# A mixed attention and gMLP kernel: Q's first tile in two halves, a finer warm-up, and new limits for the planner

## The chip, the cores and the metric

The kernel runs on one NeuronCore of a Trainium2 chip. The core has five engines that work side by side, each through its own instructions in order: TensorE (PE, with its weight loads shown apart as PEld), VectorE (DVE), ScalarE (ACT), GpSimd (POOL) and SyncE (SP), which here only issues DMAs. They wait for each other through semaphores. The metric is the device time of one execution in microseconds; lower is better. The kernel before takes 730.46 us, the median of three runs between 730.2 and 732.36.

## The reference, cut to what matters

One input x of 2048 rows and 512 columns goes through two branches, which are mixed row by row:

```python
def _A_ref(x, wq, wk, wv, wo):            # H = 32 heads, Dh = 16, one K and one V for all heads
    q = (x @ wq).reshape(B, S, H, Dh).transpose(0, 2, 1, 3)
    k = x @ wk
    v = x @ wv
    scores = jnp.einsum('bhqd,bkd->bhqk', q, k) * Dh ** (-0.5)
    p = _softmax(scores, axis=-1)
    o = jnp.einsum('bhqk,bkd->bhqd', p, v)
    return o.transpose(0, 2, 1, 3).reshape(B, S, H * Dh) @ wo

def _B_ref(x, w_in, w_sp, b_sp, w_out):   # F = 1376, Fh = 688
    z = _gelu(jnp.einsum('bsd,df->bsf', x, w_in))
    z1 = z[..., :Fh]
    z2 = _layernorm(z[..., Fh:], axis=-1)
    g = jnp.einsum('ts,bsf->btf', w_sp, z2) + b_sp[None, :, None]
    return jnp.einsum('bsf,fd->bsd', z1 * g, w_out)

g = _sigmoid((x * gate_w).sum(-1, keepdims=True))
return g * _A_ref(...) + (1 - g) * _B_ref(...)
```

Nearly all the work outside the matrix products is the softmax: 32 heads times 2048 times 2048 exponentials.

## The kernel before, in words

**Tiles.** The scores are computed with keys on the 128 partitions and queries along the free axis. A block is one product of 128 keys by 512 queries for one head; it fills one of the eight PSUM banks. Four heads of a group sit on four strips of 32 rows of the array, so four score products run side by side. A unit is 512 queries, one group of four heads and one of the two head parities: 32 units of 64 blocks (16 key tiles, four heads), 2048 blocks in all. x is loaded transposed in four chunks of 512 rows, in the order `XO = (0, 3, 2, 1)`; Q is made in 16 tiles of 128 columns by 512 queries (`g_Q`, line 463), K in chunks of 512 keys (`g_K`, line 419; the first chunk as 128 and 384), V in chunks of four key tiles (`g_V`, line 481).

**Who does the exponential.** Most blocks go to ACT: one activation (line 770) takes two or three banks out of PSUM and writes them as bf16 weights into a ring of 19 slots. The banks of its two alternating sets are 2, 3, 4 and 0, 1 (`EB`). Other blocks go to DVE, in batches of four (one key tile of one unit, four heads): it copies a block out of PSUM with a scale and an offset (`d_A`, line 782), squares it (`d_u`, line 789), and squares the result once more (`d_w`, line 795); this last step is done by DVE or by POOL, in pieces of 256 columns. Each block of DVE costs PE two products with V instead of one, and each unit gets a few correction products (`KTV`, `SVB`). DVE's blocks come through banks 5 and 4 (`DBK`); bank 4 is shared with ACT's set of three. Banks 6 (`BO`) and 7 (`BM`) hold the output sums of a unit and everything else.

**What sets the order.** The order of instructions on each engine is fixed when the program is built. A planner (from line 372) keeps a clock for PE, ACT and DVE with a fixed cost for every operation and for every arrival (the table `T`, lines 893 to 899), and always lets the engine with the earliest clock pick its next instruction (`pe_step`, `act_step`, `dve_step`; the loop is at line 1693). PE prefers scores for ACT when a set of banks is free, then score blocks for DVE, then products with V, then other work (`fill_pick`, line 1191). While the clock is below `HEAD` and the list `first` is not empty, PE takes that list's work right after the scores (lines 1414 to 1417). When PE has been too idle, the planner inserts products with zeros.

**The limits of the planner.** They stand in `PR` (line 57) and in constants above it. `RLAST` is how many blocks of the last unit must be left over when DVE takes another batch (line 989), and whether DVE may have the shared bank there (line 1376). `FLEX` is the backlog of DVE, in planned ns, below which it may take the shared bank. `WIN` is how much PSUM work DVE must have before it for POOL to be given a piece of 512 columns (line 1598) or one of its long operations (line 1589). `WRES` and `IDR`, `IDN` govern when DVE takes second products itself: it leaves `WRES` pieces of 256 columns to POOL, and when idle takes up to `IDN` pieces if at least `IDR` are there. `PRESS` is the number of free slots of the ring below which products with V are urgent.

**The head.** Memsets on DVE and POOL come first. `WARM` products on a constant tile CT (line 364) keep PE busy until x arrives. SP issues the loads of x, ACT's queue those of wk, the first quarter of wq, wv and the gate weight. DVE builds the replicated wk (line 327) and the first tile of wq (`wq_tile`, line 331), POOL the other three. The list `first` (line 902) starts with K of the first 128 keys, Q tile 0, the rest of K, and V of the chunk; the first scores need the first K piece and Q tile 0, whole.

**The tail.** When the last unit's sums are whole, DVE transposes them out of PSUM (line 807), normalises, transposes back (line 838), PE does the last output products, DVE and ACT scale, and SP sends the rows out.

Of the kernel before, what the change touches and what calls it, by code (L numbers as in the profile page):

```python
# [16 lines left out]
DH = 16  # L17
# [9 lines left out]
NMAX = 8  # L27
# [13 lines left out]
NZ = 22  # L41
WARM = 12
RLAST = 16
XO = (0, 3, 2, 1)
N0 = 3
A_OV = 63.3
HEAD = 45000.0
C_TN = 1250.0
GATE = 20000.0
# [117 lines left out]
def build_kernel(nc, x_d, wq_d, wk_d, wv_d, wo_d, win_d, wsp_d, bsp_d, wout_d, gw_d, out_d):  # L167
    es = ExitStack()
    with es:
# [83 lines left out]

        op("dve", lambda v: v.memset(CT[:], 1.0 / 64.0), w=["CT"])
        for e in range(2):
# [3 lines left out]
        op("dve", lambda v: v.memset(good[:], 1.0), w=["good"])  # L259
        op("dve", lambda v: v.memset(KTV[:], 0.0), w=["KTV"])  # L260
        op("pool", lambda g: g.memset(KN[:], 0.0), w=["KN"])
# [18 lines left out]
        def nonc(fn):  # L280
            def f(q):
                with nc.allow_non_contiguous_dma(reason="small"):
                    return fn(q)
            return f

        def ld_x(c):
# [44 lines left out]
        def wq_tile(eng, t, key, raw):  # L331
            for e in range(2):
                op(eng, lambda v, e=e: v.tensor_copy(wqd[:, :, t, :].rearrange("p a (g e d) -> p a g e d", e=2, d=DH)[:, :, :, e, :],
                                                     wq_raw[:, :, 128 * t + 64 * e:128 * t + 64 * e + 64].rearrange("p a (g d) -> p a g d", d=DH)),
                   r=[raw], w=[key])
# [4 lines left out]
        op("pool", lambda g: g.memset(bspz[:], 0.0), w=[("bspz", 0), ("bspz", 1)])  # L340
        op("pool", lambda g: g.memset(wout[32:64, 5, :], 0.0), w=["wout5"])
# [3 lines left out]
        op("pool", lambda g: g.memset(z2[:, NST * FH:], 0.0), w=["z2pad"])  # L345
        op("dve", lambda v: v.memset(sel0[:], 0.0), w=["sel0"])
        op("dve", lambda v: v.memset(sel0[:, 16:18], 1.0), w=["sel0"])
        op("dve", lambda v: v.transpose(sel[:], sel0[:]), r=["sel0"], w=["sel"])

        def mm(dst, lhsT, rhs, start, stop, r, w, tp=None, chan=None, tag=""):  # L350
# [68 lines left out]
        def g_K(c, lo=0, hi=512, e=0, b=BM):  # L419
            key = "K0a" if c == XO[0] and lo == 0 and e == 0 else ("K%d" % e, c)  # L420

            def piece(dt):
                return lambda: fm(b, hi - lo, 0, wk_r[e][:, dt, :], xT[:, dt, 512 * c + lo:512 * c + hi], dt == 0, dt == 3, [("wk_rep", e), ("x", c), ("z1", 5)], "K")

            def ev():
                op("dve", lambda v: v.tensor_copy(KA[:, e, 512 * c + lo:512 * c + hi], bank(b, hi - lo)), r=[bkey(b)], w=[key], tag="Kev")  # L426
# [36 lines left out]
        def g_Q(q, b=BM):  # L463
            c, t = q // 4, q % 4

            def piece(dt):
                return lambda: fm(b, 512, 0, wqd[:, dt, t, :], xT[:, dt, 512 * c:512 * c + 512], dt == 0, dt == 3,
                                  ["wqd0" if t == 0 else "wqd", ("x", c)], "Q")

            def ev():  # L470
                op("dve", lambda v: v.tensor_copy(QA[:, q % NQ, :], bank(b)), r=[bkey(b)], w=[("Q", q % NQ)], tag="Qev")  # L471
# [5 lines left out]
            return Group([(C_MM, piece(dt)) for dt in range(4)], [(C_EV, ev)],  # L477
                         lambda: when(("x", c), "wqd" if t else "wqd0", *([("Qdone", 2 * (q - NQ)), ("Qdone", 2 * (q - NQ) + 1)] if q >= NQ else []),
                                      *([("QSfree", q - 2)] if q >= 2 else [])), done, bank=b, tag="Q")

        def g_V(c, b=BM):
            nw = 2 * DH + 1
            kn = 4 * c + 4 > NKT - NMAX

            def piece(k, dt):
                t0 = 512 * c + 128 * k
                return lambda: fm(b, nw, 64 * k, xT[:, dt, t0:t0 + 128], wvg[:, dt, 0:nw], dt == 0, dt == 3, ["wv", "gw", "wvk", ("x", c)], "V")
            src = bank(b, 256).rearrange("p (k w) -> p k w", w=64)
# [84 lines left out]
        def g_z1(ft, tc):  # L573
            def piece(dt):
                return lambda: fm(BM, 512, 0, win[:, dt, 128 * ft:128 * ft + 128], xT[:, dt, 512 * tc:512 * tc + 512], dt == 0, dt == 3,
                                  ["win", ("x", tc)], "z1")
            ev = lambda: op("dve", lambda v: v.tensor_copy(z1[:, ft, 512 * tc:512 * tc + 512], bank(BM)), r=[bkey(BM)], w=[("z1", ft)], tag="z1ev")
            return Group([(C_MM, piece(dt)) for dt in range(4)], [(C_EV, ev)], lambda: when("win", ("x", tc)), setT(("z1", ft, tc)), tag="z1")

        def g_z2(st, h):  # L580
            def piece(dt):
                return lambda: fm(BM, 344, 0, xT[:, dt, 128 * st:128 * st + 128], win[:, dt, FH + 344 * h:FH + 344 * h + 344], dt == 0, dt == 3,
                                  ["win", ("x", st // 4)], "z2")
            ev = lambda: op("dve", lambda v: v.tensor_copy(z2[:, FH * st + 344 * h:FH * st + 344 * h + 344], bank(BM, 344)),
# [307 lines left out]

        T["wqd0"] = 6400.0
        T["wqd"] = 17000.0
        T["x0"] = 0.0
# [262 lines left out]
        def add_checks(now):  # L1158
            pu = st_["pu"]
            if pu < NU and st_["ua"] > pu:  # L1160
# [14 lines left out]
                elif "SVB" in T and not pv_const[pu]:  # L1175
                    pv_const[pu] = True
                    for g in range(4):
                        add_item(pu, g, (max(now, T["SVB"]), lambda last, g=g, n=n: o_mm(pu, g, SVB[:, NMAX - n, :], CT[:], ["SVB", "CT"], last), None, None))
            if pu < NU and pu not in chk_added:
# [59 lines left out]
        def pe_step(now):  # L1239
            r = pe_work(now)  # L1240
            if r is None:
# [4 lines left out]
                if now > 20000.0 and b < (W_GEL if gst["arm"] and gst["t"] > now - 8000.0 else pr["W_MIN"]) * W_WIN:  # L1246
# [3 lines left out]
                    if (topen is None or t_end + 40.0 <= lim) and (ds is None or ds > t_end):  # L1250
# [6 lines left out]
                        if zb is not None:  # L1257
                            for g in range(4):
                                mm(ps[32 * g:32 * g + 32, 512 * zb:512 * zb + 512], zer[:, 32 * g:32 * g + 32], CT[:], zb == BM, zb == BM, ["zer", "CT"], [bkey(zb)],
                                   tp=(0, 32 * g), chan="p" if zb == BO else None, tag="warm")  # L1260
# [36 lines left out]
        def dz_emit(cur, c_p):  # L1297
# [7 lines left out]
            if i < 20:  # L1305
                ft, tc = i // 4, i % 4
                fm(b, 512, 0, win[:, dt, 128 * ft:128 * ft + 128], xT[:, dt, 512 * tc:512 * tc + 512], dt == 0, dt == 3, ["win", ("x", tc)], "z1")
                t_end = c_p + C_MM
            else:
                tc = 2 * (i - 20) + pos // 4  # L1310
                o = 512 * b + 256 * (pos // 4)
                for q in range(4):
                    c0 = 512 * tc + 256 * (q // 2)
                    mm(ps[32 * q:32 * q + 32, o:o + 256], win[:, dt, 640 + 32 * (q % 2):672 + 32 * (q % 2)], xT[:, dt, c0:c0 + 256], dt == 0, dt == 3,
                       ["win", ("x", tc)], [bkey(b)], tp=(0, 32 * q), tag="z1")
                t_end = c_p + C_256
# [21 lines left out]
        def pe_work(now):  # L1338
# [550 lines left out]
```

## Time and profile before

| | |
|---|---|
| median of 3 runs | 730.46 us (730.2 to 732.36) |
| the profiled execution's own time | 732.71 us |
| its span, first to last instruction | 730.6 us |
| mean granted TensorE clock | 0.994 |
| busy: PE, DVE, ACT, POOL | 712.7, 704.5, 711.4, 467.0 us |
| ACT, exponentials over two banks | 725, 668.1 us busy |
| ACT, exponentials over three banks | 15, 23.1 us busy |

A row of the timeline gives the start from the beginning of the span, the duration, the engine, the line of the kernel, the operation, output and input, the shape and how many instructions were merged; a bracket gives the idle time of the engine before it and what ended that. A row of the groups gives all instructions of one line, engine and shape: count, busy time in us, mean ns of one, and the idle time before them. Almost all PE work has one line, 354, since a helper records it; there the tiles tell the groups apart.

### The profile page before, as it was taken

To read this page: it belongs to the slowest core of one execution; us is meant where nothing else is said; L and a number is where in the kernel's file an instruction comes from. 1 tells how busy PE (TensorE), PEld (TensorE's weight loads), DVE (VectorE), ACT (ScalarE), POOL (GpSimd) and SP (SyncE) were. 2 spreads that over 40 slices of the span, in tenths; PEclk is the share of its full clock that TensorE was granted. 3 is DMA by queue.
4 is the path that set the end of the run, shared out by engine and by line. 5 is a ranking of instruction groups with operands and counts; after the bars stand their busy time and mean duration, and the time that the engine had idled before them with its cause. 6 is when DMAs were issued, how large, how long until landed. Compare 5 with 4: busy or idle time off the path is not lost.

```text
span 730.6 us, 21786 instructions
## 1 busy us (share of the span) xinstructions
PE 712.7 (98%) x9037; PEld 208.4 (29%) x9037; DVE 704.5 (96%) x1035; ACT 711.4 (97%) x760; POOL 467.0 (64%) x437
## 2 busy tenths in 40 slices
PE   8999999999999999999999999999999999999995
PEld 3322333323422223222222322222232222222321
DVE  6799999999999999999999999999999999999994
ACT  5999999999999999999999999999999999999994
POOL 5834667661177777776676777767776567668660
PEclk9999999999999999999999999999999999999997
DMA  8341000000000001400000050000005000000001
GB/s 170 125 96 24 2 2 2 1 3 2 2 2 2 1 2 20 99 23 9 2 1 2 3 117 22 10 2 2 2 7 112 15 17 2 2 2 2 2 2 33
DMA packets 48609, 17.29 MB, mean 24 GB/s; under 512 B 44180, under 2 KB 47992, under 8 KB 48504
## 3 DMA queue, kind: packets, MB, share of 16 engines
q1 hardware_dynamic: 46392, 15.67, 9.3%
q8 instruction: 72, 1.18, 0.7%
q10 hardware_dynamic: 2112, 0.17, 0.2%
q14 instruction: 33, 0.27, 0.1%
HBM read 3.25 MB, written 2.10 MB: 7 GB/s over the span
## 4 chain that ended last, share of the span: by engine, by line
PE 71%; ACT 17%; DVE 6%; issue 5%; DMA 1%; ACTq 0%; DVEq 0%
PE ps L354 71%; ACT P L770 16%; DVE UW L782 2%; DVE UW L789 1%; DMA xT<-in_A_x_dram 1%; ACT z L1327 1%; DVE UW L795 1%; DVE bst L598 0%; ACT z L592 0%; DVE km L453 0%; DVE KA L426 0%; DVE T L807 0%; ACT L592 0%; DVE outsb L697 0%; DVE QA L471 0%
## 5 line engine op out<-in xcount | busy, mean ns | idle before, releaser
L770 ACT ACTIVATE P<-ps 128x1024 bf16<-128x1024 f32 (+1 forms) x741 | 686.2, 1182 | 5.9 <-PE ps L354 5.6
L795 POOL TENSOR_TENSOR UW<-UW 128x512 f16<-128x512 f16 (+1 forms) x281 | 363.5, 1294 | 161.2 <-DVE UW L795 67.3
L782 DVE TENSOR_SCALAR UW<-ps 128x512 f16<-128x512 f32 (+1 forms) x424 | 346.1, 837 | 2.5 <-PE ps L354 1.4
L354 PE MATMUL ps<-QA,KA 32*128 32x512 bf16 x2048 | 312.4, 384 | 6.1 <-ACT P L770 2.9
L354 PE MATMUL ps<-P,V 128*32 128x512 bf16 x1496 | 212.4, 385 | 0.4 <-issue 0.2
L354 PEld LDWEIGHTS ps<-QA,KA 32*128 32x128 bf16 x2048 | 84.7, 91 | 308.6 <-ACT P L770 153.5
L789 DVE TENSOR_TENSOR UW<-UW 128x2048 f16<-128x2048 f16 (+1 forms) x163 | 171.4, 1054 | 0.6
L354 PE MATMUL ps<-UW,VW 128*32 128x512 f16 x552 | 118.8, 384 | 0.0
L354 PE MATMUL ps<-wT,z 128*32 128x512 bf16 (+1 forms) x1536 | 116.2, 366 | 0.0
L795 DVE TENSOR_TENSOR UW<-UW 128x1024 f16<-128x1024 f16 (+5 forms) x167 | 108.0, 661 | 0.2
L354 PE MATMUL ps<-UW,V 128*32 128x512 f16 x552 | 84.2, 384 | 0.2 <-DVE T L807 0.2
L354 PEld LDWEIGHTS ps<-P,V 128*32 128x32 bf16 x1496 | 49.1, 94 | 57.4 <-issue 51.6
L475 POOL TENSOR_TENSOR QSQ<-QA 128x512 bf16<-128x512 bf16 x16 | 28.9, 1806 | 22.9 <-DVE z L612 7.0
L354 PEld LDWEIGHTS ps<-wT,z 128*32 128x32 bf16 x1536 | 27.7, 94 | 42.6 <-issue 42.0
L354 PEld LDWEIGHTS ps<-UW,VW 128*32 128x32 bf16 x552 | 28.1, 94 | 14.9 <-issue 11.6
L354 PE MATMUL ps<-wout,z 128*32 128x512 bf16 x384 | 31.6, 384 | 0.0
L354 PE MATMUL ps<-win,xT 128*32 128x344 bf16 x512 | 30.8, 312 | 0.1
L830 POOL TENSOR_TENSOR Tn<-T,rc 128x512 bf16<-128x512 f32 x15 | 24.6, 1639 | 6.4 <-DVE UW L782 3.1
L807 DVE STREAM_TRANSPOSE T<-ps 128x512 f32<-128x512 f32 (+1 forms) x33 | 22.6, 688 | 4.1 <-PE ps L354 4.1
L354 PE MATMUL ps<-QA,KTV 128*32 128x512 bf16 x128 | 25.0, 384 | 0.0
L354 PE MATMUL ps<-CT,SVB 128*32 128x512 bf16 x128 | 24.6, 384 | 0.0
L354 PEld LDWEIGHTS ps<-UW,V 128*32 128x32 bf16 x552 | 19.9, 94 | 15.5 <-issue 11.5
(116 smaller groups left out, 378.5 us busy)
## 6 DMA issues: line engine op xcount, KB each, us to landing
out_dram<-outsb SPq DMA_DIRECT2D x16, 128.0 KB, 1.7
win<-in_B_w_in_dram SPq DMA_DIRECT2D x1, 1376.0 KB, 6.5
wout<-in_B_w_out_dram SPq DMA_DIRECT2D x1, 640.0 KB, 4.2
wo<-in_A_wo_dram SPq DMA_DIRECT2D x8, 64.0 KB, 2.3
UW<-in_A_wq_dram SPq DMA_DIRECT2D x1, 384.0 KB, 3.8
wT<-in_B_w_sp_dram SPq DMA_TRANSPOSE x16, 4.6
UW<-in_A_wq_dram ACTq DMA_DIRECT2D x1, 128.0 KB, 3.9
wout<-in_B_w_out_dram SPq DMA_DIRECT2D x2, 48.0 KB, 1.7
```

Of the source, the lines that this page charges most:

```text
L354: return t.matmul(dst, lhsT, rhs, start=start, stop=stop, tile_position=tp)
L475: dq(pl_q, 1050.0, lambda: op("pool", lambda v: v.tensor_tensor(QSQ[:, q % 2, :], QA[:, q % NQ, :], QA[:, q % NQ, :], ALU.mult), r=[("Q", ...
L770: op("act", lambda a: a.activation(P[:, 512 * p0:512 * (p0 + n)], ps[:, 512 * b0:512 * (b0 + n)], ACT.Exp), r=[bkey(b0 + i_) for i_ in ran ...
L782: op("dve", lambda v: v.tensor_scalar(UW[:, 0, s, 512 * i:512 * (i + n)], bank(b, 512 * n), Q_A, Q_AS, ALU.mult, ALU.add), r=[bkey(b + j) ...
L789: op("dve", lambda v: v.tensor_tensor(src, src, src, ALU.mult), r=k, w=k, tag="dTT")
L795: op(eng, lambda v: v.tensor_tensor(UW[:, 1, s, 256 * a:256 * b], src, src, ALU.mult), r=[("U", s, h) for h in range(a // 2, (b + 1) // 2) ...
L807: return lambda: pgx.op("dve", lambda v: v.transpose(T1[:, jj, c0:c1], bank(BO, c1 - c0, c0)), r=[bkey(BO)], w=[("T1", jj, c0)], tag="T1")
L830: pgx.op(eng, lambda v: v.tensor_tensor(tnv[:, pr, j0:j1, b0:b1, :], t1v[:, j0:j1, b0:b1, 0:16], rc[:, j0:j1, b0:b1].unsqueeze(3).broadcas ...
L1327: op("act", lambda a: a.activation(z1f[:, 512 * i0:512 * (i0 + n)], ps[:, 512 * b0:512 * (b0 + n)], ACT.Gelu_apprx_tanh), r=[bkey(b0 + j) ...
```

## The change

Q tile 0 gets its own group `g_Q0`: two halves of 256 queries, in banks 5 and 6, each copied out by DVE on its own. The list `first` puts both halves before the rest of K, and V of the first chunk moves from bank 6 to bank 5. While no scores have been issued (`k == 0`), PE does not start a piece of that list that would, by the planner's clock, still run `HSL` = 30 ns before Q is there or later. Below `COLD` = 7000 ns such pieces are planned at twice their cost.

The warm-up becomes 43 products of 128 columns instead of 12 of 512. Its constant tile is set in two memsets, of which the warm-up needs only the first, of 128 columns. The memset of KTV moves from DVE to POOL, behind the copies of wq; on DVE the copy of wk into wvg and the three steps that make `sel` move ahead of the first wq copy. The planned arrival times and the start times of the engines are lowered. The limits RLAST, IDN, WRES, WIN, PRESS and FLEX get other values. The helper `xk` returns the same key as before.

```diff
-WARM = 12
-RLAST = 16
+WARM = 43
+RLAST = 8
+COLD = 7000.0
+HSL = 30.0
-PR = dict(HALF=100.0, IDR=10, IDN=4, WRES=16, D_HG=2500.0, D_FL=False, WIN=1000.0, WIH=560.0, BACK=32, PRESS=5, FLEX=5000.0, RMIN=32, WBL=0.5, W_MIN=0.9, HOLD=0.0, RLEND=0)
+PR = dict(HALF=100.0, IDR=10, IDN=6, WRES=10, D_HG=2500.0, D_FL=False, WIN=950.0, WIH=560.0, BACK=32, PRESS=6, FLEX=3800.0, RMIN=32, WBL=0.5, W_MIN=0.9, HOLD=0.0, RLEND=0)
...
-        op("dve", lambda v: v.memset(CT[:], 1.0 / 64.0), w=["CT"])
+        op("dve", lambda v: v.memset(CT[:, 0:128], 1.0 / 64.0), w=["CT0"])
+        op("dve", lambda v: v.memset(CT[:, 128:512], 1.0 / 64.0), w=["CT"])
...
-        op("dve", lambda v: v.memset(KTV[:], 0.0), w=["KTV"])
...
+        op("dve", lambda v: v.tensor_copy(wvg[:, :, DH:2 * DH], wk_sb[:]), r=["wk"], w=["wvk"])
+        op("dve", lambda v: v.memset(sel0[:], 0.0), w=["sel0"])
+        op("dve", lambda v: v.memset(sel0[:, 16:18], 1.0), w=["sel0"])
+        op("dve", lambda v: v.transpose(sel[:], sel0[:]), r=["sel0"], w=["sel"])
         wq_tile("dve", 0, "wqd0", "wqr0")
-        op("dve", lambda v: v.tensor_copy(wvg[:, :, DH:2 * DH], wk_sb[:]), r=["wk"], w=["wvk"])
         for t in range(1, 4):
             wq_tile("pool", t, "wqd", "wqr1")
+        op("pool", lambda v: v.memset(KTV[:], 0.0), w=["KTV"])
...
         for _ in range(WARM):
-            mm(bank(0), CT[:, 0:128], CT[:], True, True, ["CT"], [bkey(0)], tag="warm")
+            mm(bank(0, 128), CT[:, 0:128], CT[:, 0:128], True, True, ["CT0"], [bkey(0)], tag="warm")
...
+        def g_Q0(h, b):
+            def piece(dt):
+                return lambda: fm(b, 256, 0, wqd[:, dt, 0, :], xT[:, dt, 512 * XO[0] + 256 * h:512 * XO[0] + 256 * h + 256], dt == 0, dt == 3,
+                                  ["wqd0"] + xk(XO[0], 256 * h, 256 * h + 256), "Q")
+
+            def ev():
+                op("dve", lambda v: v.tensor_copy(QA[:, 0, 256 * h:256 * h + 256], bank(b, 256)), r=[bkey(b)], w=[("Q", 0)], tag="Qev")
...
-        T["wqd0"] = 6400.0
+        T["wqd0"] = 5400.0
...
-            T[("x", c)] = (6600.0, 10300.0, 15000.0, 18500.0)[i]
+            T[("x", c)] = (5950.0, 9000.0, 14000.0, 17000.0)[i]
...
-        free = {"pe": 6600.0, "act": 7000.0, "dve": 6800.0}
+        free = {"pe": 5950.0, "act": 5000.0, "dve": 5500.0}
...
-        first = deque([g_K(XO[0], 0, 128), g_Q(0, DBK[0]), g_K(XO[0], 128, 512), g_V(XO[0], BO), g_K(XO[1]), g_V(XO[1], BO), g_K(XO[2]), g_V(XO[2]),
+        first = deque([g_K(XO[0], 0, 128), g_Q0(0, DBK[0]), g_Q0(1, BO), g_K(XO[0], 128, 512), g_V(XO[0], DBK[0]), g_K(XO[1]), g_V(XO[1], BO), g_K(XO[2]), g_V(XO[2]),
...
             if head and fp is not None:
-                fill_emit(now, *fp, c_p + fp[1].pieces[fp[1].pos][0])
+                c_ = fp[1].pieces[fp[1].pos][0] * (2.0 if now < COLD else 1.0)
+                q0 = T.get(("Q", 0), 0.0)
+                if k == 0 and now < q0 < c_p + c_ - HSL:
+                    return None
+                fill_emit(now, *fp, c_p + c_)
                 st_["mode"] = "P"
-                return c_p + fp[1].pieces[fp[1].pos - 1][0]
+                return c_p + c_
```

More of the change, by code (lines that the diff above doesn't have):

```diff
@@ L284, in nonc, with xk @@
             return f
+        def xk(c, lo=0, hi=512):
+            return [("x", c)]
         def ld_x(c):
@@ L422, in piece @@
             def piece(dt):
[L423 removed]
+                return lambda: fm(b, hi - lo, 0, wk_r[e][:, dt, :], xT[:, dt, 512 * c + lo:512 * c + hi], dt == 0, dt == 3, [("wk_rep", e), ("z1", 5)] + xk(c, lo, hi), "K")
             def ev():
@@ L467, in piece @@
                 return lambda: fm(b, 512, 0, wqd[:, dt, t, :], xT[:, dt, 512 * c:512 * c + 512], dt == 0, dt == 3,
-                                  ["wqd0" if t == 0 else "wqd", ("x", c)], "Q")
+                                  ["wqd0" if t == 0 else "wqd"] + xk(c), "Q")
             def ev():
@@ L479, in g_Q, with done @@
                                       *([("QSfree", q - 2)] if q >= 2 else [])), done, bank=b, tag="Q")
+        def g_Q0(h, b):
[4 more added lines that the diff above has]
+                op("dve", lambda v: v.tensor_copy(QA[:, 0, 256 * h:256 * h + 256], bank(b, 256)), r=[bkey(b)], w=[("Q", 0)], tag="Qev")
+            def done(tm):
+                if h:
+                    T[("Q", 0)] = tm
+                    dq(pl_q, 1050.0, lambda: op("pool", lambda v: v.tensor_tensor(QSQ[:, 0, :], QA[:, 0, :], QA[:, 0, :], ALU.mult),
+                                                r=[("Q", 0)], w=[("QS", 0)], after=pg.ops["dve"][-2:-1], tag="QSQ"), tm, setT(("QS", 0)))
+            return Group([(C_256, piece(dt)) for dt in range(4)], [(335.0, ev)], lambda: when(("x", XO[0]), "wqd0"), done, bank=b, tag="Q")
         def g_V(c, b=BM):
@@ L486, in piece @@
                 t0 = 512 * c + 128 * k
-                return lambda: fm(b, nw, 64 * k, xT[:, dt, t0:t0 + 128], wvg[:, dt, 0:nw], dt == 0, dt == 3, ["wv", "gw", "wvk", ("x", c)], "V")
+                return lambda: fm(b, nw, 64 * k, xT[:, dt, t0:t0 + 128], wvg[:, dt, 0:nw], dt == 0, dt == 3, ["wv", "gw", "wvk"] + xk(c), "V")
             src = bank(b, 256).rearrange("p (k w) -> p k w", w=64)
@@ L1177, in add_checks @@
                     for g in range(4):
-                        add_item(pu, g, (max(now, T["SVB"]), lambda last, g=g, n=n: o_mm(pu, g, SVB[:, NMAX - n, :], CT[:], ["SVB", "CT"], last), None, None))
+                        add_item(pu, g, (max(now, T["SVB"]), lambda last, g=g, n=n: o_mm(pu, g, SVB[:, NMAX - n, :], CT[:], ["SVB", "CT", "CT0"], last), None, None))
             if pu < NU and pu not in chk_added:
```

14 lines of the change are left out of this document (5 added, 9 removed).

## The prediction

> **What bounds the kernel now.** I read the page's busy shares first, then busy time by stretch, then the timeline of the head and of the tail, then the groups by shape for prices.
>
> ```profile
> PE 712.7 (98%) x9037; PEld 208.4 (29%) x9037; DVE 704.5 (96%) x1035; ACT 711.4 (97%) x760; POOL 467.0 (64%) x437
> ```
>
> Three engines look full, so the shares alone do not say which one sets the end. The stretches do: columns are the stretch, its length, then busy time of PE, PEld, DVE, ACT and POOL.
>
> ```profile
> 0.00:9.27 9.27, 7.35 (x132) 3.44 (x136) 4.91 (x18) 1.28 (x1) 3.20 (x23) 1.00 0.82 159
> 9.27:30.00 20.73, 19.56 (x452) 7.43 (x443) 14.73 (x32) 20.40 (x22) 15.02 (x32) 1.00 0.63 154
> 30.00:716.02 686.02, 680.16 (x8409) 196.08 (x8405) 681.11 (x973) 685.04 (x734) 448.75 (x383) 1.00 0.08 18
> 716.02:719.92 3.90, 3.76 (x52) 0.99 (x44) 0.01 (x2) 3.41 (x4) 0.00 (x0) 1.00 0.00 0
> 719.92:730.60 10.68, 1.90 (x16) 0.47 (x16) 3.71 (x12) 1.27 (x2) 0.00 (x0) 0.58 0.18 56
> ```
>
> ACT is the bound: from its first exponential at 9.27 to its last it is idle 0.33 us in the second stretch and 0.98 us in the 686 us of the third. So the time is a head of 9.27 us, some 710 us of ACT work without gaps, and a tail of 10.7 us. DVE has slack only at the edges: 6.00 us before 30, 4.91 us in the long middle, 3.90 us at the end. Two things can move the time: the instant of the first exponential, and the number of score blocks that ACT must do, because DVE does the rest.
>
> **The head, instruction by instruction** (timeline: start, duration, engine, line, output and input; in brackets the idle time before it).
>
> ```profile
> 0.90 0.48 DVE L254 MEMSET CT<- 128x512 bf16 x1 [0.90 <-PEq L1873]
> 1.44 4.45 PE L353 MATMUL ps<-CT 128*128 128x512 bf16 x12 [1.44 <-DVE CT L254]
> 2.57 0.91 DVE L260 MEMSET KTV<- 128x1024 uint32 x1
> 5.10 0.49 DVE L333 COPY wqd<-UW 128x256 bf16<-128x256 bf16 x2 [1.41 <-DMA UW<-in_A_wq_dram]
> 6.37 0.41 PE L354 MATMUL ps<-xT,wk_rep 128*32 128x128 bf16 x16 [0.48 <-DMA xT<-in_A_x_dram]
> 6.59 1.05 PE L354 MATMUL ps<-xT,wqd 128*32 128x512 bf16 x16
> 7.14 0.29 DVE L426 CAST KA<-ps 128x128 bf16<-128x128 f32 x1 [1.05 <-PE ps L354]
> 7.48 0.83 PE L354 MATMUL ps<-xT,wk_rep 128*32 128x384 bf16 x16
> 7.69 0.69 DVE L471 CAST QA<-ps 128x512 bf16<-128x512 f32 x1 [0.26 <-PE ps L354]
> 8.14 0.71 PE L354 MATMUL ps<-wvg,xT 128*32 128x33 bf16 x56
> 8.45 0.56 DVE L426 CAST KA<-ps 128x384 bf16<-128x384 f32 x1
> 8.78 0.39 PE L354 MATMUL ps<-QA,KA 32*128 32x512 bf16 x4
> 9.27 5.28 ACT L770 ACTIVATE P<-ps 128x1536 bf16<-128x1536 f32 x5 [5.01 <-PE ps L354]
> ```
>
> The Q copy ends at 7.69 + 0.69 = 8.38, yet the first scores start at 8.78: PE, which works in order, is inside the V products. Those 0.40 us, and the length of the copy, are what this part of the change can reach.
>
> **Q in halves and the hold.** PE's work does not grow: 32 products of 256 columns instead of 16 of 512, so the second half still ends at about 6.59 + 1.05 = 7.64. The 16 extra weight loads lie beside the products, as the 16 present ones do. On DVE a copy of 256 columns lies between the rows for 128 (0.29) and 384 (0.56): 0.42 us. Behind the K copy (7.14 + 0.29 = 7.43) the first half ends at 7.85, the second at 8.27 if copies follow end to end. If they overlap by 0.08 each, as in the two-copy row below (two of 0.676 in 1.28 us), it ends at 8.12. The scores follow a DVE copy by 0.05 (K copy ends 7.43, the next K products start 7.48), hence at 8.17 to 8.32 instead of 8.78. The gain is 0.46 to 0.61 us; I take 0.5. The lower end of the range is 0, if other products still stand between Q and the scores. The hold queues the V products behind the scores. Who waits for them is DVE's V copy, and after it the first P·V products; these rows show the slack:
>
> ```profile
> 9.40 0.23 DVE L492 CAST V<-ps 128x64 bf16<-128x64 f32 x1 [0.40 <-PE ps L354]
> 10.78 0.10 PEld L354 LDWEIGHTS ps<-QA,KA 32*128 32x128 bf16 x3 [1.28 <-ACT P L770]
> 13.24 0.60 PE L354 MATMUL ps<-P,V 128*32 128x512 bf16 x5
> 11.63 0.69 DVE L426 CAST KA<-ps 128x512 bf16<-128x512 f32 x1 [1.94 <-PE ps L354]
> 19.11 0.53 POOL L509 TENSOR_SCALAR VW<-V 128x128 bf16<-128x128 bf16 x1 [1.89 <-DVE gs L495]
> ```
>
> The V copy at 9.40 has almost 4 us until 13.24, DVE idles 1.94 before 11.63, and PE's loads stand still 1.28 us before 10.78, more than the 0.71 us that V products take. So the move costs nothing. V goes from the output bank to DVE's score bank 5, which DVE first empties much later, with its first score block after 13.
>
> **Warm-up.** The first seven of the twelve products, the last three, and the weight loads (minimum, median, maximum in ns):
>
> ```profile
> 1.44 3.17 PE L353 MATMUL ps<-CT 128*128 128x512 bf16 x7 [1.44 <-DVE CT L254]
> 5.08 0.81 PE L353 MATMUL ps<-CT 128*128 128x512 bf16 x3
> L353 PEld LDWEIGHTS ps<-CT x12: 98/151/151, 1.4 to 5.3; 128*128 128x128 bf16 x12
> ```
>
> Seven in 3.17 us, the last of them lasting 0.63, are 0.42 apart. The first memset shrinks to a quarter of 0.48 us, so the warm-up starts between 0.97 and 1.44; I take 1.1. Forty-three products of 128 columns at a quarter of that pace, 0.106, take 4.6 us and end at 5.7, before x ends the wait at 6.37. This term is 0. The upper end is a pace set by the weight load, whose size does not shrink. At 0.151 us each the new products take 6.5 us, end at 7.6 and push K by 1.2 us. [...] No run here shows such products yet.
>
> **Moved setup work.** These rows carry it (the second is the SP queue):
>
> ```profile
> 13.07 0.95 POOL L340 MEMSET bspz<- 128x1024 bf16 x1
> 21.86 0.31 SPq L300 DMA_DIRECT2D bspz<-in_B_b_sp_dram  x1
> 5.87 0.21 DVE L348 STREAM_TRANSPOSE sel<-sel 128x32 f32<-128x32 f32 x1
> ```
>
> The KTV memset leaves DVE (0.91 us, hidden under the wait of 1.41 before the wq copy, so no gain) and goes to POOL behind the wqd copies. POOL's memset of half its size, bspz, takes 0.95, so about 1.9 us; it delays bspz, the four wout memsets and the first VW. The 1.89 idle before the second VW (row above) takes it up. Were that cover gone, the SVB chain would start up to 1.9 us later, with no ACT work waiting for it. The first load on SP that waits for these memsets, bspz, is issued at 21.86, and the wout loads come behind it, far after them: 0. The wvk copy and the three sel steps now run from the end of the wq copy (5.10 + 0.49 = 5.59) to 6.08; these 0.49 us move ahead of it into the same 1.41 idle, which leaves 0.92 of cover. Nobody waits for what they make until long after. No DMA is added or moved, and ACT's queue keeps its order.
>
> **The limits.** They change only which blocks DVE takes and who does the second products. Prices:
>
> ```profile
> L770 ACT ACTIVATE P<-ps 128x1024 bf16<-128x1024 f32 x725 | 668.1, 1175 | 0.5 <-PE ps L354 0.3
> L782 DVE TENSOR_SCALAR UW<-ps 128x512 f16<-128x512 f32 x296 | 191.1, 676 | 1.9 <-PE ps L354 1.2
> L782 DVE TENSOR_SCALAR UW<-ps 128x1024 f16<-128x1024 f32 x128 | 155.0, 1211 | 0.6 <-PE ps L354 0.2
> L789 DVE TENSOR_TENSOR UW<-UW 128x2048 f16<-128x2048 f16 (+1 forms) x163 | 171.4, 1054 | 0.6
> L795 DVE TENSOR_TENSOR UW<-UW 128x1024 f16<-128x1024 f16 (+5 forms) x167 | 108.0, 661 | 0.2
> 17.57 1.28 DVE L782 TENSOR_SCALAR UW<-ps 128x512 f16<-128x512 f32 x2
> ```
>
> DVE handles 296 + 2 x 128 = 552 blocks, 138 batches of four. A batch costs it (191.1 + 155.0) / 138 = 2.51 for copies out of PSUM, 171.4 / 138 = 1.24 for squares and 108.0 / 138 = 0.78 for its share of the second products: 4.53 us. It spares ACT four blocks at 668.1 / (725 x 2) = 0.461: 1.84 us. All of DVE's slack (6.00 + 4.91 + 3.90 = 14.8) would hold 14.8 / (4.53 + 1.84) = 2.3 batches: at best 4.3 us. The other end is a loss, worked out under the slow rival. Nothing in the trace shows what the new limits choose. I take half the upper end, 1.15 batches or 2.1 us, because only the 3.90 at the end, nearest to one batch, is a gap in one piece; the 4.91 is scattered over 686 us. RLAST, lowered from 16 to 8, opens just that gap: a batch in the last unit is allowed down to 12 remaining blocks instead of 20. FLEX pulls the other way, since DVE gets the shared bank only at a smaller backlog. IDN and WRES let it take second products in larger pieces and earlier, WIN lets POOL in a little more often; POOL has 64% busy, so it has room.
>
> **The sum.** The profiled execution took 732.71 us (span 730.6 plus 2.1 around it), 2.25 above the median of 730.46. 732.71 - 0.5 - 2.1 = 730.1, and by the same differences the median comes to 727.9, 0.35% faster. About 0.3%, or 2.2 us, is what a measurement can tell from no change: below 728.3 is faster, above 732.7 slower.
>
> **Rivals.**
>
> Head only: the limits redistribute work but the batch count stays, or gains and losses in the middle cancel. For it: DVE is 681.11 of 686.02 busy there, so hardly anything fits. Time 730.46 - 0.5 = 730.0. Chance 0.18.
>
> The last unit overruns. The place is the wait of DVE's final transpose:
>
> ```profile
> 713.73 2.29 DVE L795 TENSOR_TENSOR UW<-UW 128x1024 f16<-128x1024 f16 x3
> 719.92 0.45 DVE L807 STREAM_TRANSPOSE T<-ps 128x256 f32<-128x256 f32 x1 [3.90 <-PE ps L354]
> 711.43 1.00 POOL L795 TENSOR_TENSOR UW<-UW 128x256 f16<-128x256 f16 x1 [0.97 <-DVE UW L795]
> 693.13 26.30 ACT L770 ACTIVATE P<-ps 128x1024 bf16<-128x1024 f32 x27
> ```
>
> ACT ends at 719.43 and DVE at 716.02. One late batch more brings DVE to 720.55 and ACT to 717.6: the end moves 0.6 us later although ACT is done sooner. Two bring DVE to 725.1, or to 723.5 if idle POOL takes their cubes (2 x 0.78): 3.6 to 5.2 later, less 0.5 of the head, 733.5 to 735.1. It decides from 6.6 us of extra DVE work in the last unit (3.90 + 0.5 + 2.2). For it: POOL ends at 712.43, and an extra batch must wait on PE, ACT's banks and two squarings in series. Against: batches may come earlier in the unit, where they fit. Chance 0.21, time 733.5.
>
> The warm-up overruns x at the weight-load pace: 1.2 later, less the 0.5: 731.2. Against it: in the present trace the load of the next product runs during the current one. Chance 0.06.
>
> The clock is still low when K and Q arrive. Now the last three warm products fill 0.81 us from 5.08, against 0.42 + 0.42 + 0.63 = 1.47 for three at the first pace, so the pace had doubled by then, 3.6 us after the start. If small products do not open it, K and Q need 0.22 + 0.86 more, less the 0.5: 731.0. [...] Chance 0.07.
>
> **How the numbers follow.** Forecast 0.48 (faster, own range 725.6 to 728.3), head only 0.18, warm-up and clock 0.13 (within), overrun 0.21 (slower). The low end is head plus the full slack, 730.46 - 0.5 - 4.3 = 725.6. The high end, 733.0, takes in the mild part of the overrun and leaves its rest, some 0.15, outside.
>
> **What would show it.** First exponential at 8.7 to 8.9 instead of 9.27, its scores right behind the second Q copy, V products after them. DVE score blocks 556 to 560 instead of 552, ACT busy about 2 us less. DVE's wait before the final transpose shorter than 3.90 but not gone; if that transpose starts later than 719 with PE released by DVE's second products, the overrun is true. First K products at 6.3 to 6.4 and 0.22 ahead of Q: warm-up harmless. The prediction is wrong if the block count falls, or if ACT shows idle time in the long middle stretch beyond 0.98 us because the new order has scores late.

## The result, and the profile after

The changed kernel takes 734.55 us, median of 7 runs (733.26 to 735.89), against 730.44 us (730.14 to 732.36) for the kernel before. The ratio is 1.0051, 95% interval 1.0039 to 1.0063: slower by half a per cent. The forecast was 727.9, the range 725.6 to 733.0; both were missed.

One thing about the profile of before has to be said first. The execution that it shows took 732.71 us, and its surplus over the median lies at its very end. Both kernels were profiled once more: before again took 730.1 us with a span of 728.2, the changed kernel again 735.08 with 733.2. The work between the first and the last exponential of before is the same in both of its profiles; only the stretch behind the last exponential shrank from 11.17 to 8.83 us. So the typical profile of before is the second one, and these are its stretches (stretch, length, then busy time of PE, PEld, DVE, ACT and POOL, the granted clock, DMA share, GB/s):

```profile
0.00:9.19 9.19, 7.75 (x132) 3.50 (x136) 4.91 (x18) 1.28 (x1) 3.20 (x23) 1.00 0.89 171
9.19:31.00 21.81, 20.63 (x467) 7.75 (x456) 15.03 (x33) 21.48 (x22) 16.02 (x33) 1.00 0.62 149
31.00:719.37 688.37, 682.48 (x8440) 196.96 (x8429) 680.91 (x973) 687.38 (x736) 447.17 (x382) 1.00 0.08 17
719.37:728.20 8.83, 1.73 (x18) 0.43 (x18) 3.71 (x12) 1.26 (x2) 0.00 (x0) 0.68 0.21 68
```

The changed kernel (its first profile), with the second stretch cut in four:

```profile
0.00:8.96 8.96, 7.24 (x152) 6.40 (x155) 4.11 (x19) 1.28 (x1) 3.23 (x23) 1.00 0.88 151
8.96:10.55 1.59, 1.59 (x95) 1.09 (x80) 0.61 (x4) 1.59 (x2) 0.00 (x0) 1.00 2.30 253
10.55:12.42 1.87, 0.00 (x1) 0.00 (x0) 0.53 (x1) 0.35 (x1) 0.38 (x1) 1.00 0.46 91
12.42:20.04 7.62, 7.04 (x78) 1.62 (x81) 4.32 (x9) 5.44 (x5) 6.91 (x13) 0.56 0.89 116
20.04:31.00 10.96, 10.42 (x294) 4.19 (x288) 8.32 (x19) 10.91 (x12) 7.24 (x16) 1.00 0.48 158
31.00:722.53 691.53, 685.36 (x8446) 197.20 (x8445) 681.65 (x950) 690.88 (x739) 464.92 (x386) 1.00 0.08 18
722.53:731.20 8.67, 3.00 (x55) 1.08 (x45) 3.71 (x12) 1.27 (x3) 0.00 (x0) 0.94 0.23 71
```

The first exponential comes 0.23 us sooner (8.96 against 9.19). From there to 31 us, ACT is idle for 21.81 - 21.48 = 0.33 us in before. In the changed kernel it is idle for 3.75 us, the lengths of the third, fourth and fifth rows less its busy time there: 1.52 while PE does nothing at all for 1.87 us, 2.18 in the stretch whose granted clock is 0.56, and 0.05 after that. That is 3.42 us more. Over the whole span up to the tail ACT has 0.31 us more work, behind 31 it has 0.34 less idle time, and the tail is 0.16 shorter. -0.23 + 3.42 + 0.31 - 0.34 - 0.16 = 3.0, the difference of the spans. In the changed kernel's second profile PE stood longer, ACT was idle 22.03 - 17.47 = 4.56 us in that stretch, and the spans differ by 5.0. The medians, 4.1 apart, lie between the two.

The timeline of PE shows the place (start, duration, line, operation, shape, count, and the idle time before):

```profile
6.49 0.41 PE L359 MATMUL ps<-xT,wk_rep 128*32 128x128 bf16 x16 [0.68 <-DMA xT<-in_A_x_dram]
6.71 1.06 PE L359 MATMUL ps<-xT,wqd 128*32 128x256 bf16 x32
8.27 0.26 PE L359 MATMUL ps<-wvg,xT 128*32 128x33 bf16 x16
8.47 0.39 PE L359 MATMUL ps<-QA,KA 32*128 32x512 bf16 x4
10.09 0.46 PE L359 MATMUL ps<-wvg,xT 128*32 128x33 bf16 x31
12.42 0.27 PE L359 MATMUL ps<-wvg,xT 128*32 128x33 bf16 x13 [1.87 <-issue]
12.62 0.39 PE L359 MATMUL ps<-QA,KA 32*128 32x512 bf16 x3
```

The 31 and the 13 V products belong to one group of 64, which reads the same chunk of x and writes the same bank. Each product is issued as four strips, so by these counts the pause falls between the third and the fourth strip of one product. Nothing they read can have been late for the one and not for the other, and the profile calls the wait "issue": no event ended it. The place points to their code. The profile lists two DMA queues of the kind "instruction", q8 and q14, and the packets of q8 keep step with PE, as is shown further down:

```profile
q8 instruction: 73, 1.20, 0.7%
```

73 packets of 16,384 bytes go with 2 x 9080 = 18,160 recorded products and weight loads of PE, near 250 a packet. Counted in order of time, with the few events that PE records beside them, the pause lies right behind PE's 449th recorded instruction. In the trace's records of that queue the first packet starts at 10.08 us and is put down as ending at 11.09; PE goes on at 12.42. From the start of the tenth packet to that of the sixtieth, PE records 256.1 instructions a packet, in the first profile of before as in that of the changed kernel. Below, a block is what one packet brings, taken as 256 instructions by this count.

What ACT does meanwhile, and the half-speed stretch that follows:

```profile
8.96 1.94 ACT L790 ACTIVATE P<-ps 128x1536 bf16<-128x1536 f32 x2 [4.70 <-PE ps L359]
13.11 3.44 ACT L790 ACTIVATE P<-ps 128x1536 bf16<-128x1536 f32 x3 [2.21 <-PE ps L359]
17.01 1.02 ACT L790 ACTIVATE P<-ps 128x1024 bf16<-128x1024 f32 x1 [0.46 <-PE ps L359]
18.59 1.02 ACT L790 ACTIVATE P<-ps 128x1024 bf16<-128x1024 f32 x1 [0.56 <-PE ps L359]
20.04 10.62 ACT L790 ACTIVATE P<-ps 128x1024 bf16<-128x1024 f32 x10 [0.43 <-PE ps L359]
```

The wait of 2.21 us that ends at 13.11 is the pause and the 0.69 us that the scores behind it still need; the three waits after it, 0.46, 0.56 and 0.43, fall into the stretch of low clock and make 1.45.

And DVE's score blocks, and the wait before its final transpose:

```profile
L802 DVE TENSOR_SCALAR UW<-ps 128x512 f16<-128x512 f32 x294 | 189.6, 677 | 6.1 <-PE ps L359 5.6
L802 DVE TENSOR_SCALAR UW<-ps 128x1024 f16<-128x1024 f32 x129 | 156.2, 1211 | 2.9 <-PE ps L359 2.5
723.24 0.78 DVE L827 STREAM_TRANSPOSE T<-ps 128x256 f32<-128x256 f32 x2 [0.74 <-PE ps L359]
```

294 + 2 x 129 = 552 blocks: the new limits move no batch from ACT to DVE. By the planner's own list they let DVE take six batches of the last unit instead of five, 138 in all as before, and DVE ends close to ACT without holding it up.

### The profile page after: what moved, and what is told of

Read it like the earlier page. It is cut to its first block, busy times and chain, and to the rows that moved or that the text cites. A ratio compares the mean times of both kernels' runs of the same rounds, so it can differ in the third digit from the quotient of the medians.

```text
span 731.2 us, 21823 instructions
## 1 busy us (share of the span) xinstructions
PE 714.7 (98%) x9080; PEld 211.6 (29%) x9080; DVE 703.3 (96%) x1010; ACT 711.7 (97%) x760; POOL 482.7 (66%) x436
## 4 chain that ended last, share of the span: by engine, by line
PE 66%; ACT 20%; DVE 7%; issue 6%; DMA 1%; ACTq 0%; DVEq 0%
PE ps L359 66%; ACT P L790 19%; DVE UW L802 3%; DVE UW L815 1%; DVE UW L809 1%; DMA xT<-in_A_x_dram 1%; ACT z L1346 1%; DVE bst L618 0%; ACT z L612 0%; DVE T L827 0%; DVE KA L431 0%; DVE km L458 0%; ACT L612 0%; DVE QA L476 0%; ACTq L157 0%
## 5 line engine op out<-in xcount | busy, mean ns | idle before, releaser
L815 POOL TENSOR_TENSOR UW<-UW 128x512 f16<-128x512 f16 (+1 forms) x279 | 378.3, 1356 | 152.4 <-DVE UW L802 62.3
L359 PE MATMUL ps<-P,V 128*32 128x512 bf16 x1496 | 205.5, 386 | 0.0
L815 DVE TENSOR_TENSOR UW<-UW 128x1024 f16<-128x1024 f16 (+6 forms) x144 | 104.8, 736 | 0.0
L359 PE MATMUL ps<-UW,V 128*32 128x512 f16 x552 | 77.8, 384 | 0.2 <-DVE T L827 0.2
L359 PEld LDWEIGHTS ps<-P,V 128*32 128x32 bf16 x1496 | 47.6, 94 | 48.3 <-issue 43.9
L480 POOL TENSOR_TENSOR QSQ<-QA 128x512 bf16<-128x512 bf16 x15 | 26.6, 1774 | 20.9 <-PE ps L359 7.8
```

The costliest lines, as they stand in the source:

```text
L359: return t.matmul(dst, lhsT, rhs, start=start, stop=stop, tile_position=tp)
L815: op(eng, lambda v: v.tensor_tensor(UW[:, 1, s, 256 * a:256 * b], src, src, ALU.mult), r=[("U", s, h) for h in range(a // 2, (b + 1) // 2) ...
```

## The experiments

Two theories stood against each other. The code theory: PE comes to the end of the loaded code before the next block is there, and the clock falls after the pause. The order theory: the new limits and the new order are slower by themselves, and the pause is only where it shows.

**The warm-up, and the bare number of instructions.** Three kernels. In the first the changed kernel gets its old warm-up back:

```diff
-WARM = 43
+WARM = 12
...
-            mm(bank(0, 128), CT[:, 0:128], CT[:, 0:128], True, True, ["CT0"], [bkey(0)], tag="warm")
+            mm(bank(0), CT[:, 0:128], CT[:], True, True, ["CT", "CT0"], [bkey(0)], tag="warm")
```

> The changed kernel with the old warm-up of 12 products of 512 columns (62 fewer PE instructions); everything else, the planned order too, as changed. Code theory (PE runs out of loaded instructions at its 449th recorded instruction, 62 instructions sooner than it would with the old warm-up): the stall of 1.87 us on PE near 10.5 us shrinks below 0.8, the granted clock stays full from 10 to 20 us, ACT's idle time between 9 and 30 us falls from 3.7 to under 1, and the time comes to 729.5 to 731.5. Order theory (the new limits and the new order are slower by themselves): 734.5 within 0.7.

In the second the kernel before gets the new warm-up (43 products of 128 columns and the split memset), in the third as many products of which 9 are long:

```diff
-WARM = 12
+WARM = 9
...
             mm(bank(0), CT[:, 0:128], CT[:], True, True, ["CT"], [bkey(0)], tag="warm")
+        for _ in range(34):
+            mm(bank(0, 32), CT[:, 0:128], CT[:, 0:32], True, True, ["CT"], [bkey(0)], tag="warm")
```

> The kernel before with the new warm-up alone: 43 products of 128 columns, their tile set by its own memset. Code theory: the same stall appears in the old order, PE stands 1 us or more at its 449th instruction, and the time rises to 731.5 to 734. Order theory: 730.4 within 0.7, since the warm-up ends before x lands in either form.

> The kernel before with 9 products of 512 columns and 34 of 32 columns as warm-up: as many PE instructions as in the changed kernel, but the tensor engine kept busy mostly by long products. Code theory: as for the small products, 731.5 to 734, because only the count matters. If it is the shape of the warm-up products (the clock opening late behind small ones), 730.4 within 0.7, and only the 43 products of 128 are slow.

Measured: the old warm-up in the changed kernel 734.46 us (ratio to before 1.0052, 1.0036 to 1.0069), no gain. The new warm-up in the kernel before 733.21 (1.0032, 1.0020 to 1.0045); the padded one 733.24 (1.0036, 1.0022 to 1.0050). So 62 more instructions of PE (31 products, each with its weight load) cost the old order 2.7 us, in both shapes of the products, and the clock's opening behind small products is not it. The pause stands at the same count in all three. Two rows each of the changed kernel with the old warm-up, of before with the new one, and of before itself (its second profile):

```profile
11.81 0.20 PE L359 MATMUL ps<-wvg,xT 128*32 128x33 bf16 x4
14.32 0.23 PE L359 MATMUL ps<-wvg,xT 128*32 128x33 bf16 x8 [2.31 <-issue]
```

```profile
11.98 0.48 PE L355 MATMUL ps<-wvg,xT 128*32 128x33 bf16 x42
13.36 0.32 PE L355 MATMUL ps<-wvg,xT 128*32 128x33 bf16 x22 [0.89 <-issue]
```

```profile
13.16 0.60 PE L354 MATMUL ps<-P,V 128*32 128x512 bf16 x5
13.95 0.39 PE L354 MATMUL ps<-P,V 128*32 128x512 bf16 x2 [0.19 <-issue]
```

My expectation for the first of the three was wrong, and the trace tells why. With fewer instructions PE reaches its 449th later, but the block comes later too. This table is from the traces. "Goes on" is the start of the 450th recorded instruction, and "256 earlier" that of the 194th, where by the count of 256 a packet PE passes from one block to the next:

| kernel | 256 earlier | packet of code | reaches 449th | goes on | pause |
|---|---|---|---|---|---|
| before | 8.49 | 11.60 to 12.54 | 13.47 | 14.03 | 0.56 |
| before, again | 8.41 | 11.48 to 12.40 | 13.39 | 13.95 | 0.56 |
| before, 43 small products | 8.38 | 10.75 to 11.90 | 12.28 | 13.36 | 1.08 |
| before, 9 long and 34 short | 8.43 | 11.15 to 12.35 | 12.33 | 13.55 | 1.22 |
| changed | 7.62 | 10.08 to 11.09 | 10.38 | 12.42 | 2.04 |
| changed, again | 7.63 | 10.38 to 11.57 | 10.38 | 12.98 | 2.60 |
| changed, old warm-up | 8.64 | 11.69 to 12.82 | 11.82 | 14.32 | 2.50 |

The pause here runs from start to start of two instructions. In each row PE goes on 1.2 to 1.6 us after the recorded end of the packet and 4.8 to 5.7 us after it passed the mark 256 earlier. What differs is how fast it eats those 256 instructions: 5.0 us before, 3.9 in the two with a longer warm-up, 2.8 to 3.2 in the changed order. So it is the rate, not the count alone. The code theory stands, with that correction. In all ten profiles that pause here, those below with other limits or a held load included, the pause lies behind the same number of recorded instructions; before has it too, in small.

**Fewer instructions, same products.** Each V product, four strips of 32 columns of weights, is issued once over 128 columns:

```diff
-                return lambda: fm(b, nw, 64 * k, xT[:, dt, t0:t0 + 128], wvg[:, dt, 0:nw], dt == 0, dt == 3, ["wv", "gw", "wvk"] + xk(c), "V")
+                return lambda: mm(bank(b, nw, 64 * k), xT[:, dt, t0:t0 + 128], wvg[:, dt, 0:nw], dt == 0, dt == 3, ["wv", "gw", "wvk"] + xk(c), [bkey(b)], tag="V")
```

> The changed kernel, warm-up included, with each V product issued once over 128 columns of weights instead of as four strips of 32: 32 PE instructions for a chunk of V instead of 128. Code theory: PE reaches its 449th instruction only after the next block of code has landed, no stall there, clock full, 727.5 to 729.5. Order theory: 734.5 within 1, or a little slower because the V products no longer run four abreast.

> The kernel before with each V product issued once over 128 columns of weights instead of in four strips. Code theory: its own small stall of 0.56 us at the 449th instruction goes too, 729.5 to 730.4. If the gain of the same edit in the changed kernel came from V products that are better placed or cheaper, and not from the code, it gains as much here: 727 to 728.5. If whole products cost PE time that matters: over 731.

Measured: 730.67 us in the changed kernel (ratio 1.0008, 0.9991 to 1.0024), by the medians 3.9 us less than with strips, by the ratios 3.1; three of its ten runs took 732.8 to 733.6, and why is not shown. In the kernel before 731.22 (1.0005, 0.9993 to 1.0018), no gain: above the 729.5 to 730.4 that was expected there, and by its median in the branch in which whole products cost time, though the interval leaves that open. In the changed kernel PE reaches the 449th instruction at 17.43, five us after the 12.42 at which it goes on there with strips, and does not pause; the clock stays full and ACT runs through:

```profile
15.00:20.00 5.00, 4.87 (x63) 1.73 (x59) 4.97 (x12) 5.00 (x6) 3.81 (x8) 1.00 0.78 253
9.58 17.64 ACT L790 ACTIVATE P<-ps 128x1536 bf16<-128x1536 f32 x17 [5.32 <-PE ps L359]
```

That the edit is worth 3.9 us in one order and nothing in the other speaks for the code and against cheaper V products. The time stays above the 727.5 to 729.5 that was expected, and the first exponential of this profile, 9.58, is late for a reason of its own: V, which stands before it, waited for the gate weight, whose load landed 6.5 us after its issue instead of 4.7.

**The limits.** RLAST and the line of limits of before put into the changed kernel, and the new ones into the kernel before:

```diff
-RLAST = 8
+RLAST = 16
...
-PR = dict(HALF=100.0, IDR=10, IDN=6, WRES=10, D_HG=2500.0, D_FL=False, WIN=950.0, WIH=560.0, BACK=32, PRESS=6, FLEX=3800.0, RMIN=32, WBL=0.5, W_MIN=0.9, HOLD=0.0, RLEND=0)
+PR = dict(HALF=100.0, IDR=10, IDN=4, WRES=16, D_HG=2500.0, D_FL=False, WIN=1000.0, WIH=560.0, BACK=32, PRESS=5, FLEX=5000.0, RMIN=32, WBL=0.5, W_MIN=0.9, HOLD=0.0, RLEND=0)
```

> The changed kernel with the limits of before (RLAST, IDN, WRES, WIN, PRESS, FLEX); halves, hold, warm-up and arrival times as changed. Code theory: the stall on PE at the 449th recorded instruction stays at 1.5 to 2.5 us, since the list of the head is what brings PE there early, and the time stays at 733.5 to 736. Limits theory: without the new limits the loss goes, 729.5 to 731.

> The kernel before with the new limits alone. Code theory: PE reaches its 449th instruction as late as before, stands there 0.6 us or less, and the time is 729 to 731. Limits theory: 733 to 736. If one batch more for DVE were what the limits bring, 728.5.

> The changed kernel with whole V products and the limits of before: the head of the change without the stall and without the limits. If the limits are worth about one batch (1.8 us), 732 to 733 against 730.7 with the new ones; if they are worth nothing, 730.2 to 731.2; if they cost, under 730. ACT's first exponential between 8.9 and 9.6 us in each case.

Measured: the changed kernel with the old limits 736.97 us (1.0097, 1.0080 to 1.0114), 2.4 slower than with the new ones. The pause stays, as expected (PE idle 2.43 us), but the time is above the 733.5 to 736 that went with it. The kernel before with the new limits 733.82 (1.0050, 1.0031 to 1.0069), 3.7 slower than with its own in the same round; that is the answer of the limits theory, 733 to 736, and not the 729 to 731 of the code theory. With whole V products and the old limits 733.45 (1.0058, 1.0035 to 1.0081), 2.8 slower than with the new ones, its runs 731.27 to 736.19; the 732 to 733 expected for a gain of one batch is near, but DVE does 552 blocks in every version, so no batch is behind it. So the limits are no gain in themselves: by the medians, each set does better in the order it came with. Where the old limits lose in the new order was not followed up. The old order with the new limits shows the loss that the prediction had as its slow rival. ACT ends at 711.15 + 9.05 = 720.20, DVE works on until 722.59, and the final transpose starts at 723.09:

```profile
711.15 9.05 ACT L770 ACTIVATE P<-ps 128x1024 bf16<-128x1024 f32 x9
721.20 0.67 DVE L789 TENSOR_TENSOR UW<-UW 128x1024 f16<-128x1024 f16 x1
721.90 0.69 DVE L795 TENSOR_TENSOR UW<-UW 128x1024 f16<-128x1024 f16 x1
723.09 0.78 DVE L807 STREAM_TRANSPOSE T<-ps 128x256 f32<-128x256 f32 x2 [0.49 <-PE ps L354]
```

That is 2.9 us from the last exponential to the transpose, against 0.5 in before and 0.7 in the changed kernel. In this kernel the V products come in the old places, PE reaches its 449th instruction at 13.85 and goes straight on, and no stretch of low clock follows before the tail (1.00 from 9.87 to 720.20): its loss is not the pause.

**What makes the block late.** Two loads that run at that time, held back one at a time in the changed kernel: the last two chunks of x, each issued only when the load before it has landed, and the 384 KB of wq, moved behind the last chunk.

```diff
-            sp_dma(lambda q: q.dma_start_transpose(xT[:, :, 512 * c:512 * c + 512], x2[512 * c:512 * c + 512, :]), w=[("x", c)], chain=False, tag="x%d" % c)
+            sp_dma(lambda q: q.dma_start_transpose(xT[:, :, 512 * c:512 * c + 512], x2[512 * c:512 * c + 512, :]), w=[("x", c)], chain=c in XO[2:], tag="x%d" % c)
```

```diff
-            if i == 1:
-                sp_dma(lambda q: q.dma_start(wq_raw[:, :, 128:512], wq_d[:, 128:512].rearrange("(dt p) n -> p dt n", p=128)), w=["wqr1"], chain=False)
+            if i == 3:
+                sp_dma(lambda q: q.dma_start(wq_raw[:, :, 128:512], wq_d[:, 128:512].rearrange("(dt p) n -> p dt n", p=128)), w=["wqr1"], chain=True)
```

> The changed kernel with the last two chunks of x issued only when the load before each has landed. What delays the block of code that PE waits for at its 449th instruction? If it is the transposing loads of these chunks: PE resumes there before 11 us instead of 12.4, the clock stays full until the chunks are needed, ACT's idle time before 31 us falls from 3.75 to 1 to 2 (the later x may cost some again), 731 to 733.5. If the transposes do not matter: PE resumes at 12.0 to 12.6, and later x makes it 735 or more.

> The changed kernel with the 384 KB load of the rest of wq moved from between the x chunks to behind the last one. If this load is what delays the block of code, PE resumes at its 449th instruction before 11 us and the time is 731 to 733; if the x transposes delay it, PE resumes at 12 us or later, as they then come sooner into the same stretch, and the time is 734 to 736.

Measured: 734.40 us (1.0054, 1.0038 to 1.0069) and 734.41 (1.0059, 1.0038 to 1.0080), no gain. With x held back the packet starts at 9.44 and PE goes on at 11.90; with wq held back at 8.95 and 11.44. Both come somewhat sooner than in the changed kernel (12.42 and 12.98), by half a microsecond to 1.5. That is one profile each, and the two of the changed kernel differ by 0.56, so the share of x is not clear of that. 4.0 to 4.3 of the 4.8 to 5.4 us remain, and both kernels fall to the low clock, 0.5. Both expectations asked for a sharper answer, PE before 11 us, and got none.

The traces do show how that time divides. PE's packets keep step with its count: over all fourteen profiles, the tenth to the thirtieth packet start a median 0.05 us after PE passes a further multiple of 256 instructions behind the 194th, nine in ten of them within 0.65 us of it. By this, in these traces, a packet starts when PE passes into the block before the one that it brings. The first packet, the one PE waits for here, starts late: 2.2 to 3.1 us after its mark in most profiles, 1.80 with x held back, 1.49 with wq held back, and 0.41 in before with whole V products, where PE passes the mark only at 11.01. It takes 0.9 to 1.2 us, and where PE waits for it, PE goes on 1.2 to 1.6 us after its end. What holds the first packet back, and what the last piece is, stays open.

The two repeated profiles had these expectations:

> The changed kernel once more. PE stands 1.5 to 2.5 us at its 449th recorded instruction again, the clock is at half speed for some 7 us from 13 to 14 us on, and ACT is idle 3 to 4.5 us before 31 us.

> The kernel before once more. PE stands less than 0.7 us at its 449th instruction and the clock stays full. If the 11.2 us from the last exponential to the end of the span in the profile shown belong to a slow end of that one execution, here they are 8.3 to 10.

Both held in substance. In the first the figures lie at the upper edge or just past it: PE idle 2.42 us, ACT 4.56, the low clock from 14.64 on (0.85 as the mean from 8.97 to 31). In the second, before's pause of 0.56 us is a code pause as well, as the table shows.

## Why the prediction was wrong

- **Q in halves and the hold**: right in mechanism and nearly in size. The scores start 1.98 us after the first K product instead of 2.41, 0.43 sooner, where 0.46 to 0.61 was worked out. x landed later in the changed kernel's profiles, so 0.2 to 0.3 us are left at the first exponential. The hold did not clear the way fully: 16 V products still ran before the scores.
- **"So the move costs nothing"**: this is the step that failed. It asked who waits for the V products and found slack for their result. It did not ask what stands behind them in PE's own instruction stream. The new order runs both Q halves, the rest of K, V, the next K and half of the next V within 4 us, eats 256 instructions in 2.8 us, and by the code theory meets the end of its loaded code. In place of nothing the runs showed a pause of PE of 1.87 and 2.42 us, a stretch of low clock behind it, and 3.42 us more idle time of ACT in the first profile. The step's own row of 1.28 us in which PE's loads stand still before 10.78 was read as room; by the table it was also time in which the code could come. No run took back the hold, the halves or the place of V alone, so their shares in the faster pace are not shown.
- **Warm-up, term 0**: right in time, the small products take 4.77 us, 0.106 apart, and end at 5.81, before x; the rival of the weight load's pace did not come true. That the rival of the late clock did not is luck in part: the trace's clock records begin, at 1.00, at 6.46 us, 0.03 before the first K product, and at 4.41 in the second profile. In the first profile of before they begin at 4.90, and there the warm-up products go from 0.43 to 0.22 us apart. In the profile of before with the new limits the first record stands at 7.37, behind the old, long warm-up. There Q starts 0.41 us after K instead of 0.22, and the first exponential is late, at 9.87. And the 62 further instructions are not free in every order: 2.7 us in the old one, none in the new.

```profile
6.67 0.62 PE L354 MATMUL ps<-xT,wk_rep 128*32 128x128 bf16 x16
7.08 1.18 PE L354 MATMUL ps<-xT,wqd 128*32 128x512 bf16 x16
```

- **The limits, 2.1 us for 1.15 batches**: wrong. The blocks are 552 as before. The trace of before could not show it, and the half of an upper bound was no measurement. In the new order they are better than the old ones by 2.4 us, for a reason that was not followed up.
- **The overrun of the last unit**: not in the changed kernel, where DVE's wait before the transpose is 0.74 us, shorter than 3.90 but not gone, as foreseen for the good case. It is real where the same limits meet the old order.
- **Head only, 730.0**: this is what is left when the pause is taken away, 730.67 measured with whole V products. The pause goes with that edit, and the low clock behind it, and 3.9 of the 4.1 us by the medians; no rival had the pause.

Neither of the prediction's signs of being wrong came: the block count did not fall, and behind 31 us ACT is idle for only 0.65 us. The loss lay ahead of where they looked. No version here beats the kernel before clearly; the changed order with whole V products equals it.

## What to carry to other kernels

When work is moved forward on an engine that runs unrolled code, count the instructions and not only the time. Here many short products in a row, 256 recorded instructions in 2.8 us where before took 5.0, met a pause of 2.04 us, by the code theory because they outran the loading of the code. In the profile it stands as 1.87 us of idle time "issue" in the middle of a group that waits for nothing. The same arithmetic in fewer, wider instructions removed it, at 730.67 us against 734.55. Limits that were chosen for one order are to be tried again with each order, and never carried over as a gain.

## What the runs showed of the hardware

A pause of PE of 1 to 2.6 us early in the kernel was followed by 3.4 or 6.8 us at a granted clock of 0.5 in all eight profiles with such a pause (the two of the changed kernel, the three with its warm-up, x or wq edited, the one with the old limits, and the two of before with more instructions in the warm-up). Behind the 0.56 us of before the clock stayed full, 1.00 up to 719.37 in its second profile. In the changed kernel the low clock cost ACT 1.45 us in three waits, beside the 2.21 of the pause itself. The low stretches are 3.41 or 6.83 us long. Each of them starts 6.83 or 10.24 us after the trace's first clock record, and that record lies anywhere from 3.77 to 7.37 us in the fourteen profiles.

The clock fell without a pause of code too. In the profile of before with whole V products PE reaches its 449th instruction only at 23.79, yet the clock is low, 0.5, from 13.51 to 20.33, and ACT is idle 1.81 us up to 31; why the clock fell there was not tried. So that the pause makes the clock fall is likely, and not shown.

```profile
13.00:20.50 7.50, 7.43 (x54) 1.34 (x55) 4.87 (x9) 5.76 (x6) 3.68 (x7) 0.54 0.77 230
```

Around the end of the first packet of code, put down at 10.08 to 11.09 in the changed kernel, the other loads nearly stand (last column, GB/s):

```profile
10.50:11.00 0.50, 0.05 (x2) 0.00 (x0) 0.50 (x1) 0.40 (x1) 0.00 (x0) 1.00 0.17 2
11.00:11.50 0.50, 0.00 (x0) 0.00 (x0) 0.08 (x1) 0.00 (x0) 0.00 (x0) 1.00 0.08 8
12.00:12.50 0.50, 0.08 (x12) 0.08 (x13) 0.00 (x0) 0.00 (x0) 0.40 (x2) 1.00 1.28 291
```

In before the same lull is at 12.50 to 13.00, 23 GB/s, with its packet put down as ending at 12.54, and 290 follow from 13.50 on. Which of the two holds up the other is not shown.
